# Fused attention and mixture of experts: the first expert's weight split planned behind the last gather, and a newly searched order of the experts' stage

## The chip, the cores and the metric

The kernel runs on one core of a Trainium2 chip. The metric is device time in microseconds (us) of one execution, the median of several. Engines: TensorE (PE; its weight loads are PEld), VectorE (DVE), ScalarE (ACT), GpSimd (POOL), and SyncE (SP), which issues most of the DMAs.

## The reference, cut to what matters

Two attentions feed a mixture of experts. The part that the change touches is the second function; its input `x` is the attention's output.

```python
def sm_attn(qq, kk, vv):            # softmax(scale * q k^T) v
    ...
p_packed = sm_attn(p, k, v)         # 8 x 8 heads, 32 packed rows
x = sm_attn(q, p_packed, p_packed)  # 8 x 8 heads, 576 rows -> 4608 tokens x 512

def _moe_ref(x, w_gate, w1, w2):
    N, D, E, cap = 4608, 512, 8, 576
    order = np.argsort(-(x @ w_gate).flatten())
    for idx in order:               # best (token, expert) pairs first
        tok, e = idx // E, idx % E
        if assigned[tok] >= 0 or counts[e] >= cap:
            continue
        assigned[tok] = e
        counts[e] += 1
    for e in range(E):              # w1[e]: 512 x 1024, w2[e]: 1024 x 512
        h = np.maximum(x[assigned == e] @ w1[e], 0)
        out[assigned == e] = h @ w2[e]
```

Each of the 8 experts gets exactly 576 tokens.

## The kernel before, in words

**Attention** runs first, in 16 groups of four heads. It writes `x` to DRAM (`xd`) and leaves the gate's logits on the chip (`Lg`). The change does not touch it.

**The router** finds the experts one after another, in the order in which they fill up. For expert n it masks what is taken (`close_a`, `close_b`, `build_a` to `build_v`), then narrows a threshold by counting steps: 2 for the first expert, 9 for the second, 11 for the others up to the seventh. One step is two counts on ScalarE (`count_a`, L868) and one on VectorE (`count_v`, L873), their sum over partitions on TensorE (`count_m`, L879 and L880), and the new threshold on VectorE (`upd_a`, L885, and `upd_b`, L894). `bound_m`, `test_m` and `assign` close the search. Then the list of the expert's 576 tokens is made: `slot_a` to `slot_v` and `onehot` on VectorE, the list products `list_m` (L1037) and `list_s` (L1049) on TensorE, and `list_b` (L1056), which leaves the indices in `gi`.

**An expert's rows** are fetched in five `gather`s (L1067), indirect DMAs that GpSimd issues: four of 128 rows and one of 64. For experts 0 to 2, TensorE transposes each piece (`xt_p`, L1100, into `px`), ScalarE rounds it to a high part `xh` (`xt_h`, L1106), and VectorE takes the low part `xl` from it (`xt_l`, L1111). For later experts the rows go through DRAM and VectorE transposes them (`xt_t` L1082, `xs_h`, `xs_l` L1094).

**An expert's weights** come in four quarters q, each a piece of `w1` and a piece of `w2` of 512 KB. SyncE loads them (`load`, L1120 and L1124), ScalarE makes the high part (`split_h`, L1129), and `split_l` (L1135) the low part. `split_l` is on GpSimd, in four instructions, but for the first quarter of expert 0, where VectorE does it in one instruction a piece. The loaded piece has two buffers, so quarter q + 2 can be loaded only when both splits of quarter q are done.

**The products** are f32 in three terms. `f1` (L1148) makes `hp` for one of eight slices f of the hidden size and one half m of the tokens: 4 matmuls of w1h by xh, 4 of w1h by xl, 4 of w1l by xh. `h_hi` (ACT, L1154) and `h_lo` (DVE, L1159) split the result, and `f2` (L1168 to L1173) adds to the five output tiles `y`. `ev` and `scatter` (L1201) write the rows out. `hp`, `px` and all small router products share three PSUM banks.

**The order** of all this is made when the program is built. Every operation of the experts' stage is entered in a planner (`Later`, a list scheduler) with an engine, a length (`LEN`), what it depends on, and a priority (a due time plus an entry of `TURN` for its kind and expert). The planner takes the operation that can start first; among those of one engine that can start at once it takes the one with the lowest priority. `SPARE` adds time between an operation on another engine and the named one. What comes out is the order in which each engine's queue is filled. Dependencies that stand only in the planner put nothing into the program: at run time an engine takes its queue in order and waits only where data or buffers ask for it. The planner thinks a gather landed 2.0 us after its issue plus .6 us, with 1.26 us between gathers, and puts `xt_p`, `xt_h`, `xt_l` some 1.6 us behind that.

Of the kernel before, what the change touches and what calls it, by code (L numbers as in the profile page):

```python
# [24 lines left out]
NTS = {1: 9}  # L25

LEN = {
    'assign': .4, 'bound': .08, 'bound_a': .1, 'bound_m': .14, 'build_a': 1.08, 'build_b': .72, 'build_k': 1.2, 'build_s': .13,
    'build_t': .15, 'build_v': .34, 'check_a': 1.6, 'check_m': .06, 'check_t': .6, 'close_a': .42, 'close_b': .48,
    'count_a': 1.2, 'count_m': .08, 'count_v': .44, 'ev': .48, 'ev_b': .6, 'expert': .09, 'f1': .533, 'f2': .7, 'f2x': .468,  # L30
    'gather': 1.26, 'h_hi': .31, 'h_lo': .38, 'list_a': .22, 'list_b': .6, 'list_m': .56, 'list_s': .22, 'load': .42,
    'member': .15, 'onehot': .67, 'scatter': 1.3, 'slot_a': .11, 'slot_b': .08, 'slot_c': .25, 'slot_d': .12, 'slot_e': .42,
    'slot_f': .42, 'slot_v': 1.4, 'split_h': .96, 'split_l': 2.8, 'test_c': .45, 'test_k': .28, 'test_m': .12, 'test_t': .2,
    'upd_a': .16, 'upd_b': .15, 'upd_c': .38, 'xg_ld': .5, 'xg_st': .38, 'xs_h': .42, 'xs_l': .47, 'xt_h': .48, 'xt_l': .6,
    'xt_p': .42, 'xt_t': .78}
# [243 lines left out]
def attention(ctx, tc, q, k, v, p, wg, xd, Lg, ident, wz, on_pool, early, late):  # L279
# [313 lines left out]


TURN = {
    'assign': (-9929.2, -1406.843, 695.138, 8016.483, 10766.841, 22037.982),
    'bound': (-3834.6, 19907.391, 1545.019, -15480.779, -5390.105, -3834.6),
    'bound_a': (0.0, -12064.251, -9565.382, -20090.433, -17648.964, 0.0),
    'bound_m': (0.0, -17844.652, -20096.332, -29653.072, -12440.691, 0.0),
    'build_a': (-2008.2, 18667.7, -18971.318, -5313.609, -5894.946, -2008.2),  # L600
    'build_b': (-2483.5, -7489.825, -13194.366, -4933.016, 4459.692, -2483.5),
    'build_k': (13240.5, 6770.915, 135183.815, 144824.42, 127860.865, 13240.5),
    'build_s': (0.0, -5506.748, 49376.469, 41829.641, 44711.332, 0.0),
    'build_t': (-9387.6, 18308.204, -24260.41, -19414.757, -22539.789, -9387.6),
    'build_v': (-8683.2, 3735.557, 34884.663, 34875.733, 36679.642, -8683.2),
    'check_a': (-3104.3, -3104.3, -3104.3, -3104.3, -3104.3, 25290.017),
    'check_m': (-3944.6, -3944.6, -3944.6, -3944.6, -3944.6, -8346.239),
    'check_t': (-3790.1, -3790.1, -3790.1, -3790.1, -3790.1, 3123.699),
    'close_a': (126.2, -22548.492, 259.466, 2123.26, 8359.189, 11624.021),
    'close_b': (-1960.4, 6234.801, 9449.371, 3539.501, 27866.288, -1960.4),  # L610
    'count_a': (-10221.0, 8707.999, -9829.586, -32227.368, -17557.572, -10221.0),
    'count_m': (-3687.4, 1429.069, -33012.921, -22925.971, -14518.958, -3687.4),
    'count_v': (-10658.5, -15050.716, -12417.95, 8192.386, -7906.393, -10658.5),
    'ev': (-5552.944, -3688.201, 6558.093, 8280.19, -10046.237, 13097.729),
    'ev_b': (-15492.946, 5184.873, 34456.107, 21302.216, 13334.529, -10138.807),
    'expert': (3457.5, -8328.201, 58298.188, 43236.934, 48338.711, 37867.42),
# [7 lines left out]
    'list_m': (16650.6, 15144.715, 2587.43, -12792.414, -3772.509, -20818.002),
    'list_s': (0.0, 27317.24, 3051.717, -3202.607, -457.014, 35078.358),
    'load': (24326.573, 97.039, -13710.125, -20482.231, -12447.259, 122.969),
    'member': (2847.3, 14117.27, 35484.901, 34707.856, 10795.168, 58872.233),
    'onehot': (-25997.2, -8211.351, -6183.93, -1931.135, 6932.093, -5368.273),
    'scatter': (10143.091, -36084.19, -8418.517, -10134.109, 5366.606, -12148.254),
    'slot_a': (-9633.1, -16932.437, 6718.434, -3983.583, -17178.811, -18985.786),  # L630
    'slot_b': (2288.0, -27923.294, 16326.799, -5139.904, 19811.628, -5998.061),
    'slot_c': (3152.9, -12181.673, 1877.318, -21791.852, -7757.971, -7053.733),
    'slot_d': (-1573.9, 29902.664, -5261.31, -22598.46, 12155.618, 8876.647),
    'slot_e': (-524.5, 2159.212, 37652.808, 34413.836, 34668.615, -8031.793),
    'slot_f': (7834.8, 15849.014, -9822.272, -628.14, -7972.32, 10427.988),
    'slot_v': (4056.3, 63995.495, 8187.024, -4230.816, 8863.725, 32775.272),
    'split_h': (3302.957, 59748.569, -127700.582, -128978.441, -133757.296, 20644.281),
    'split_l': (-7655.334, -5499.444, 36.831, 21635.26, 20988.04, 9614.49),
    'test_c': (1962.7, -53079.145, 3397.318, -7627.982, -17958.568, 1962.7),
    'test_k': (-9416.6, 18359.967, -60537.576, -65842.54, -78645.049, 6810.101),  # L640
    'test_m': (5327.7, 3430.116, -27468.576, -16199.522, -18112.833, 5327.7),
    'test_t': (-12609.4, -16891.226, 32800.306, 35251.939, 23245.714, -12609.4),
    'upd_a': (-7827.8, -25855.316, -15537.501, -3920.09, -18452.757, -7827.8),
    'upd_b': (1841.6, 13191.368, -13839.699, 7546.071, 18546.542, 1841.6),
    'upd_c': (40.5, -7739.416, 48363.268, 30737.669, 31194.472, 40.5), 'warm': (5018.43, 4200.7, 4200.7, 4200.7, 4200.7, 4200.7),
    'xg_ld': (-9296.7, -9296.7, -36445.1, -50675.93, -40479.904, 2433.332),
    'xg_st': (-1329.6, -1329.6, 3510.5, -3634.894, 20385.538, -26436.257),
    'xs_h': (-3606.4, -3606.4, -7756.0, -12318.781, 5109.768, -9563.927),
    'xs_l': (-45.1, -45.1, 19770.7, 16501.78, 19786.225, 3883.391),
    'xt_h': (-1214.368, -55658.344, 28097.803, 19354.6, 19354.6, 1824.8),  # L650
    'xt_l': (-4458.649, -10492.511, 30711.146, 15800.4, 15800.4, -9835.7),
    'xt_p': (-17602.312, 1842.144, 53034.826, 52713.8, 52713.8, 1446.9),
    'xt_t': (2153.2, 2153.2, -22396.6, -31796.512, -13888.503, -1010.97),}


def router_constants(nc, cst, tmp):
# [72 lines left out]
def experts(ctx, tc, rt, tmp, xd, xs, Lg, w1, w2, out, ident, wz, before):  # L729
# [549 lines left out]
    def u(k, f):  # L1279
        return 6.46 * (8 * k + f)  # L1280
# [15 lines left out]
    for n in range(E):  # L1296
# [5 lines left out]
        elif n:  # L1302
# [279 lines left out]
```

## Time and profile before

| what | value |
|---|---|
| median of 3 runs (lowest to highest) | 637.77 us (637.51 to 638.63) |
| the profiled execution | 643.15 us |
| its span, first to last instruction | 641.4 us |
| TensorE busy | 594.6 us (93%) |
| VectorE / ScalarE / GpSimd busy | 412.9 / 336.1 / 368.5 us |
| first `f1` matmul of expert 0 | 176.66 us |

The profile is one execution taken by the hardware profiler, with times from its first instruction. Attention fills about the first 148 us, the first expert's routing lies between 148 and 165 us, and the experts' stage after it. A busy TensorE need not be at its peak: matmuls are pipelined.

### The profile page before, as it was taken

Reading aid. Unit: us, or ns where it says so; the run is one execution under the profiler, and the core shown is the slowest. Engines: PE = TensorE matmul, PEld = TensorE weight load, DVE = VectorE, ACT = ScalarE, POOL = GpSimd, SP = SyncE. Lnnn points to the kernel's source line nnn. Section 1 sums busy time; section 2 is a strip of 40 time slices with the busy share of each in tenths; the row PEclk is TensorE's granted clock in tenths of the full one; section 3 lists DMA queues with packets and bytes.
Section 4 is the critical chain, followed back from the end, with each engine's and each line's share of the span. In section 5 each row is a group of like instructions: output and inputs, shape, how many; then the busy total and the mean of one; then the engine's idle time right before and its main releaser. Section 6 shows DMA issues by size and latency. Waiting matters only on the chain. (4 is left out here: it accounts for less than half of the span.)

```text
span 641.4 us, 12439 instructions
## 1 busy us (share of the span) xinstructions
PE 594.6 (93%) x4099; PEld 496.7 (77%) x4101; DVE 412.9 (64%) x1508; ACT 336.1 (52%) x853; POOL 368.5 (57%) x592
## 2 busy tenths in 40 slices
PE   6999899983699999999899999998999999999996
PEld 3678677752388888888788788797888989889984
DVE  7899999997666767657557966964792144162111
ACT  5677777762383774764664565385334235233102
POOL 8378676680570793962954783675447756725003
PEclk9899999997999999999999999999999999999998
DMA  8999996332820634432566365438333864812002
GB/s 274 369 341 309 296 319 198 111 112 75 269 68 6 226 107 150 155 108 76 196 231 155 132 214 116 141 137 245 103 100 107 261 157 144 241 44 75 1 1 78
DMA packets 76953, 103.42 MB, mean 161 GB/s; under 512 B 11792, under 2 KB 57104, under 8 KB 76880
## 3 DMA queue, kind: packets, MB, share of 16 engines
q1 hardware_dynamic: 70464, 83.64, 41.2%
q0 software_dynamic: 5888, 18.88, 8.5%
q8 instruction: 35, 0.57, 0.4%
q14 instruction: 38, 0.31, 0.2%
q10 hardware_dynamic: 528, 0.02, 0.1%
HBM read 77.74 MB, written 24.77 MB: 160 GB/s over the span
## 5 line engine op out<-in xcount | busy, mean ns | idle before, releaser
L1159 DVE SCALAR_TENSOR_TENSOR h<-hp,h 128x288 fp32r<-128x288 f32 (+2 forms) x192 | 59.5, 351 | 116.3 <-ACT h L1154 111.8
L1135 POOL TENSOR_TENSOR w2l<-w2s,w2h 128x256 fp32r<-128x256 f32 x124 | 92.0, 773 | 68.6 <-ACT w2h L1129 68.5
L1135 POOL TENSOR_TENSOR w1l<-w1s,w1h 128x256 fp32r<-128x256 f32 x124 | 91.1, 767 | 58.2 <-ACT w1h L1129 51.6
L1168 PE MATMUL y<-w2h,h 128*128 128x512 f32 x256 | 104.5, 408 | 0.0
L1170 PE MATMUL y<-w2h,h 128*128 128x512 f32 x256 | 101.0, 395 | 0.0
L1169 PE MATMUL y<-w2l,h 128*128 128x512 f32 x256 | 101.0, 395 | 0.0
L1148 PE MATMUL hp<-xh,w1h 128*128 128x288 f32 x512 | 91.5, 301 | 4.6 <-DVE h L1159 1.7
L1148 PE MATMUL hp<-xl,w1h 128*128 128x288 f32 x512 | 90.6, 299 | 0.6 <-DVE xl L1111 0.3
L1154 ACT ACTIVATE h<-hp 128x288 fp32r<-128x288 f32 x128 | 48.7, 406 | 80.4 <-issue 37.4
L1148 PE MATMUL hp<-xh,w1l 128*128 128x288 f32 x512 | 90.4, 298 | 0.0
L1148 PEld LDWEIGHTS hp<-xh,w1h 128*128 128x128 f32 x512 | 77.1, 188 | 10.8 <-DVE h L1159 1.7
L868 ACT ACTIVATE ja<-Vt,nT 128x288 bf16<-128x288 f32 x118 | 63.2, 536 | 36.7 <-DVE nT L894 34.5
L1148 PEld LDWEIGHTS hp<-xl,w1h 128*128 128x128 f32 x512 | 74.9, 188 | 1.3 <-DVE xl L1111 0.5
L1201 POOL DMA_INDIRECT out_dram<-xg,gi x40 | 39.1, 979 | 63.7 <-DVE fl L1427 36.9
L1148 PEld LDWEIGHTS hp<-xh,w1l 128*128 128x128 f32 x512 | 74.6, 188 | 0.1
L1129 ACT CAST w1h<-w1s 128x1024 fp32r<-128x1024 f32 x32 | 33.5, 1047 | 56.2 <-DMA w1s<-in_moe_w_dram 17.8
L1067 POOL DMA_INDIRECT xg<-xd,gi x40 | 39.0, 975 | 32.4 <-DVE Lw L989 21.7
L1170 PEld LDWEIGHTS y<-w2h,h 128*128 128x128 f32 x256 | 48.0, 187 | 11.5
L1169 PEld LDWEIGHTS y<-w2l,h 128*128 128x128 f32 x256 | 48.1, 188 | 8.2
L1168 PEld LDWEIGHTS y<-w2h,h 128*128 128x128 f32 x256 | 48.0, 188 | 8.3
L1129 ACT CAST w2h<-w2s 128x1024 fp32r<-128x1024 f32 x32 | 33.5, 1048 | 32.4 <-issue 13.3
L543 PE MATMUL xp<-P,th 128*128 128x264 f32 (+1 forms) x154 | 37.1, 329 | 7.0 <-ACT xs L553 4.5
(269 smaller groups left out, 1146.1 us busy)
## 6 DMA issues: line engine op xcount, KB each, us to landing
w1s<-in_moe_w_dram SPq DMA_DIRECT2D x32, 512.0 KB, 6.0
w2s<-in_moe_w_dram SPq DMA_DIRECT2D x32, 512.0 KB, 4.3
kl<-in_k_dram SPq DMA_DIRECT2D x16, 576.0 KB, 5.4
ql<-in_q_dram SPq DMA_DIRECT2D x16, 576.0 KB, 6.2
vl<-in_v_dram SPq DMA_DIRECT2D x32, 256.0 KB, 5.2
xd<-xs SPq DMA_DIRECT2D x32, 256.0 KB, 3.3
xg<-xs SPq DMA_DIRECT2D x20, 288.0 KB, 6.3
xs<-xg SPq DMA_DIRECT2D x20, 256.0 KB, 3.8
```

The costliest lines, as they stand in the source:

```text
L543: nc.tensor.matmul(xp[:m, :264], T[a, g][:, o:o + m], T[w, g], start=i == 0, stop=i == 2)
L868: nc.scalar.activation(ja, Vf, AF.Sign, bias=S_['nT'][:, j:j + 1], scale=-1.0, accum_out=cp[:, j:j + 1])
L1067: nc.gpsimd.indirect_dma_start(out=X['xg', k, c][:m], out_offset=None, in_=xd, in_offset=bass.IndirectOffsetOnAxis(ap=X['gi', k][:m, c:c + ...
L1129: nc.scalar.copy(X[n + 'h', k, q], X[n + 's', k, q])
L1135: eng.tensor_sub(X[n + 'l', k, q][r], X[n + 's', k, q][r], X[n + 'h', k, q][r].bitcast(F32))
L1148: nc.tensor.matmul(X['hp', k, f, n], X[W, k, q][:, d, 128 * r:128 * r + 128], X[Z, k][:, d, 288 * n:288 * n + 288], start=i + d == 0, stop ...
L1154: nc.scalar.activation(X['h', k, f][:, 288 * n:288 * n + 288], X['hp', k, f, n], AF.Relu)
L1159: V.scalar_tensor_tensor(h[:, o:o + b - a], p[:, a - 288 * n:b - 288 * n], 0.0, h[:, a:b].bitcast(F32), op0=OP.max, op1=OP.subtract)
L1168: nc.tensor.matmul(y, hh, wh, start=f == 0, stop=False)
L1169: nc.tensor.matmul(y, hh, wl, start=False, stop=False)
L1170: nc.tensor.matmul(y, hl, wh, start=False, stop=f == 7)
L1201: s = nc.gpsimd.indirect_dma_start(out=out, out_offset=bass.IndirectOffsetOnAxis(ap=X['gi', k][:m, t:t + 1], axis=0), in_=X['yo', k, t][:m ...
```

## The change

Three edits. First, the planner is told that `split_l` of expert 0's first quarter (the one on VectorE) depends on the last gather of expert 0; until now only the second and later quarters did. Second, lengths and spare times: the small products on TensorE are entered as .06 to .08 us longer, and .3 us of spare time is put in front of `count_m`, `bound_m`, `test_m`, `slot_a`, `slot_c`, `list_m`, `list_s` and `build_t`, .05 us in front of `f2`. Third, nearly all entries of `TURN` are new, the result of a search over orders with these settings. No instruction is added or removed; what changes is the order in each queue. The diff, cut to its core (58 lines of `TURN` have new numbers; four are shown):

```diff
 LEN = {
-    'assign': .4, 'bound': .08, 'bound_a': .1, 'bound_m': .14, 'build_a': 1.08, 'build_b': .72, 'build_k': 1.2, 'build_s': .13,
-    'build_t': .15, 'build_v': .34, 'check_a': 1.6, 'check_m': .06, 'check_t': .6, 'close_a': .42, 'close_b': .48,
-    'count_a': 1.2, 'count_m': .08, 'count_v': .44, 'ev': .48, 'ev_b': .6, 'expert': .09, 'f1': .533, 'f2': .7, 'f2x': .468,
+    'assign': .4, 'bound': .08, 'bound_a': .1, 'bound_m': .21, 'build_a': 1.08, 'build_b': .72, 'build_k': 1.2, 'build_s': .13,
+    'build_t': .22, 'build_v': .34, 'check_a': 1.6, 'check_m': .12, 'check_t': .6, 'close_a': .42, 'close_b': .48,
+    'count_a': 1.2, 'count_m': .14, 'count_v': .44, 'ev': .48, 'ev_b': .6, 'expert': .09, 'f1': .533, 'f2': .7, 'f2x': .468,
...
-SPARE = {'f1': .1, 'xt_p': .3}
+SPARE = {'f1': .1, 'f2': .05, 'xt_p': .3, 'count_m': .3, 'bound_m': .3, 'test_m': .3, 'slot_a': .3, 'slot_c': .3, 'list_m': .3, 'list_s': .3, 'build_t': .3}
...
-    'f1': (5538.963, 10905.075, 3567.902, -11602.304, -575.199, 10364.904),
-    'f2': (124988.012, 96881.814, 3574.469, -3442.054, 753.66, 15591.93),
+    'f1': (22829.595, 17476.141, -598.159, -17684.53, 8822.542, 16946.171),
+    'f2': (128367.327, 85925.544, -590.941, 1590.706, 15430.256, 20714.866),
...
-    'split_l': (-7655.334, -5499.444, 36.831, 21635.26, 20988.04, 9614.49),
+    'split_l': (-8891.522, 5752.33, 15284.995, 36562.132, 41772.256, 15822.959),
...
-    'xt_l': (-4458.649, -10492.511, 30711.146, 15800.4, 15800.4, -9835.7),
+    'xt_l': (-13398.275, -4227.517, 20493.449, 15800.4, 15800.4, -9835.7),
...
-                op(('split_l', n, q, w), e, d, zq, lambda n=n, q=q, w=w, eng=eng: split_l(n, q, w, eng), [('split_h', n, q, w)] + ([('gather', 0, 4)] if n == 0 and q else []))
+                op(('split_l', n, q, w), e, d, zq, lambda n=n, q=q, w=w, eng=eng: split_l(n, q, w, eng), [('split_h', n, q, w)] + ([('gather', 0, 4)] if n == 0 and q < 2 else []))
```

Read closely, the condition also changes for quarters 2 and 3 of expert 0: with `q` they were tied to the last gather, with `q < 2` they are not. Both follow quarter 1 on GpSimd, which stays tied.

## Rows read from the trace of the kernel before

**Rows 1.** Stretches of time: length, PE, PEld, DVE, ACT, POOL busy, PEclk, DMA.

```profile
176.60:629.60 453.00, 441.95 (x2773) 386.05 (x2773) 254.54 (x1076) 220.89 (x522) 249.06 (x349) 1.00 0.42 131
```

**Rows 2.** The same view in stretches of 16 us.

```profile
160.00:176.00 16.00, 10.31 (x56) 5.13 (x56) 10.43 (x28) 5.36 (x6) 8.76 (x10) 0.91 0.79 267
...
400.00:416.00 16.00, 14.94 (x83) 12.37 (x83) 15.86 (x34) 6.62 (x12) 9.74 (x13) 1.00 0.41 133
```

**Rows 3.** Timeline of PE at expert 0's start: start, duration, what, idle before.

```profile
169.77 0.63 PE L1100 MATMUL px<-ident,xg 128*128 128x128 f32 x4 [1.83 <-DVE wm L835]
...
175.33 0.66 PE L1100 MATMUL px<-ident,xg 128*128 128x128 f32 x4 [0.87 <-DMA xg<-xd,gi]
...
176.66 0.79 PE L1148 MATMUL hp<-xh,w1h 128*128 128x288 f32 x4
...
178.38 0.69 PE L1148 MATMUL hp<-xh,w1l 128*128 128x288 f32 x4
```

**Rows 4.** Timeline of POOL: the five gathers of expert 0.

```profile
166.00 1.20 POOL L1067 DMA_INDIRECT xg<-xd,gi  x1 [21.65 <-DVE Lw L989]
167.51 1.67 POOL L1067 DMA_INDIRECT xg<-xd,gi  x1 [0.30 <-issue]
169.48 1.04 POOL L1067 DMA_INDIRECT xg<-xd,gi  x1 [0.30 <-issue]
170.82 0.95 POOL L1067 DMA_INDIRECT xg<-xd,gi  x1 [0.30 <-issue]
172.07 0.91 POOL L1067 DMA_INDIRECT xg<-xd,gi  x1 [0.30 <-issue]
```

**Rows 5.** Timeline of DVE in the same stretch.

```profile
167.12 1.22 DVE L1135 TENSOR_TENSOR w1l<-w1s,w1h 128x1024 fp32r<-128x1024 f32 x1
168.25 1.22 DVE L1135 TENSOR_TENSOR w2l<-w2s,w2h 128x1024 fp32r<-128x1024 f32 x1
...
170.10 0.45 DVE L840 TENSOR_TENSOR ck<-eq,k 128x288 f32<-128x288 f32 x1
...
177.02 0.68 DVE L1111 TENSOR_TENSOR xl<-px,xh 128x512 fp32r<-128x512 f32 x1
```

**Rows 6.** Timeline of POOL: first and last of a later expert's five gathers.

```profile
496.47 0.98 POOL L1067 DMA_INDIRECT xg<-xd,gi  x1 [0.16 <-issue]
...
501.53 0.91 POOL L1067 DMA_INDIRECT xg<-xd,gi  x1 [0.30 <-issue]
```

**Rows 7.** Timeline of SP: loads of expert 0's quarters 2 and 3.

```profile
168.36 0.38 SPq L1120 DMA_DIRECT2D w1s<-in_moe_w_dram  x1
...
175.80 0.37 SPq L1120 DMA_DIRECT2D w1s<-in_moe_w_dram  x1
```

**Rows 8.** DMA queue of the gathers, 167.8 to 169.4 us: packets, MB, share.

```profile
q0 software_dynamic: 80, 0.26, 55.0%
```

**Rows 9.** DMA queue of the loads, 169.4 to 171.0 us.

```profile
q1 hardware_dynamic: 437, 0.45, 88.3%
```

**Rows 10.** Timeline of DVE beside a busy POOL, at 306 us.

```profile
306.24 0.99 DVE L840 TENSOR_TENSOR ck<-eq,k 128x288 f32<-128x288 f32 x1
```

**Rows 11.** Timeline of PE: expert 0's first f2, and its f1 for f = 4.

```profile
189.84 0.39 PE L1168 MATMUL y<-w2h,h 128*128 128x512 f32 x1
...
198.83 0.70 PE L1148 MATMUL hp<-xh,w1h 128*128 128x288 f32 x4
```

**Rows 12.** What PE waited for (176.6 to 640 us): total, times, longest.

```profile
PE pc L879 <- ACT ja L868: 3.8, 4, 2.4
...
PE pl L1037 <- DVE Bv L1027: 1.3, 2, 1.1
```

**Rows 13.** What DVE waited for, the same columns.

```profile
DVE g L885 <- remote: 5.7, 2, 4.4
```

**Rows 14.** Timeline of ACT: the first evacuation of expert 0's output.

```profile
243.11 0.58 ACT L1179 COPY xg<-y 128x512 f32<-128x512 f32 x1
```

**Rows 15.** Timeline of PE: the first f1 of expert 1.

```profile
234.10 0.80 PE L1148 MATMUL hp<-xh,w1h 128*128 128x288 f32 x4
```

More of the change, by code (lines that the diff above doesn't have):

```diff
@@ L27 @@
 LEN = {
[L28 to L33 removed]
+    'assign': .4, 'bound': .08, 'bound_a': .1, 'bound_m': .21, 'build_a': 1.08, 'build_b': .72, 'build_k': 1.2, 'build_s': .13,
+    'build_t': .22, 'build_v': .34, 'check_a': 1.6, 'check_m': .12, 'check_t': .6, 'close_a': .42, 'close_b': .48,
+    'count_a': 1.2, 'count_m': .14, 'count_v': .44, 'ev': .48, 'ev_b': .6, 'expert': .09, 'f1': .533, 'f2': .7, 'f2x': .468,
+    'gather': 1.26, 'h_hi': .31, 'h_lo': .38, 'list_a': .22, 'list_b': .6, 'list_m': .62, 'list_s': .3, 'load': .42,
+    'member': .15, 'onehot': .67, 'scatter': 1.3, 'slot_a': .18, 'slot_b': .08, 'slot_c': .32, 'slot_d': .12, 'slot_e': .42,
+    'slot_f': .42, 'slot_v': 1.4, 'split_h': .96, 'split_l': 2.8, 'test_c': .45, 'test_k': .28, 'test_m': .19, 'test_t': .2,
     'upd_a': .16, 'upd_b': .15, 'upd_c': .38, 'xg_ld': .5, 'xg_st': .38, 'xs_h': .42, 'xs_l': .47, 'xt_h': .48, 'xt_l': .6,
@@ L595 @@
 TURN = {
[L596 to L616, printed above, removed]
@@ L624 @@
[L624 to L630, printed above, removed]
@@ L651 @@
-    'xt_l': (-4458.649, -10492.511, 30711.146, 15800.4, 15800.4, -9835.7),
-    'xt_p': (-17602.312, 1842.144, 53034.826, 52713.8, 52713.8, 1446.9),
-    'xt_t': (2153.2, 2153.2, -22396.6, -31796.512, -13888.503, -1010.97),}
+    'assign': (-9929.2, 8021.767, 1598.018, 25071.993, 15905.586, 19528.151),
+    'bound': (-3834.6, 33362.577, 23308.579, -14054.897, 4294.231, -3834.6),
+    'bound_a': (0.0, -23099.862, -18927.01, -6646.28, -7446.145, 0.0),
+    'bound_m': (0.0, -16262.41, -25858.1, -29606.998, -6444.35, 0.0),
@@ new lines @@
+    'build_a': (-2008.2, 13932.591, -19234.405, 477.463, -21918.238, -2008.2),
+    'build_b': (-2483.5, 6419.326, -19940.965, -13355.792, -3326.46, -2483.5),
+    'build_k': (13240.5, 21336.957, 103092.436, 142588.696, 138208.467, 13240.5),
+    'build_s': (0.0, -1424.652, 62993.037, 30494.077, 42436.465, 0.0),
+    'build_t': (-9387.6, 15342.024, -22513.891, -35046.8, -27715.647, -9387.6),
+    'build_v': (-8683.2, -5257.386, 26835.481, 34680.713, 39948.709, -8683.2),
+    'check_a': (-3104.3, -3104.3, -3104.3, -3104.3, -3104.3, 43347.295),
@@ new lines @@
+    'check_m': (-3944.6, -3944.6, -3944.6, -3944.6, -3944.6, -6322.488),
+    'check_t': (-3790.1, -3790.1, -3790.1, -3790.1, -3790.1, -15637.835),
+    'close_a': (126.2, -19872.0, 3529.0, -4647.709, 16010.75, 15146.648),
+    'close_b': (-1960.4, 13714.184, 9752.643, 6162.018, 35035.524, -1960.4),
+    'count_a': (-10221.0, 34463.865, -16869.524, -38255.921, -13828.885, -10221.0),
+    'count_m': (-3687.4, 19119.637, -21950.979, -25841.009, -13216.544, -3687.4),
+    'count_v': (-10658.5, -18579.112, -1973.712, 15307.119, -3064.439, -10658.5),
@@ new lines @@
+    'ev': (-5262.78, 8732.876, -3312.21, 13749.653, 2483.229, 8455.869),
+    'ev_b': (-20778.526, 10758.981, 42803.284, 19365.779, 12982.825, -25592.823),
+    'expert': (3457.5, -12565.341, 59526.876, 36408.156, 55063.13, 37630.649),
+    'f1': (22829.595, 17476.141, -598.159, -17684.53, 8822.542, 16946.171),
+    'f2': (128367.327, 85925.544, -590.941, 1590.706, 15430.256, 20714.866),
+    'gather': (-19807.898, -17526.384, 26831.228, 6211.744, 16258.338, -10318.461),
+    'h_hi': (-7203.688, 8190.046, -24358.184, -32127.244, -38725.715, 1091.569),
@@ new lines @@
+    'h_lo': (144985.247, 36211.178, -120910.825, -129786.648, -102869.948, -8767.126),
+    'list_a': (-5736.9, 3506.348, -2894.641, -21125.526, -5240.8, 11358.32),
+    'list_b': (-4287.7, -4602.215, 21828.469, 21153.02, 10476.004, -2393.23),
+    'list_m': (16650.6, -1866.812, 8825.717, -12769.88, -20082.349, -27825.146),
+    'list_s': (0.0, 31015.054, -1423.308, -8724.485, -2031.368, 43162.251),
+    'load': (29195.964, -5213.228, -20105.183, -22848.27, 10482.923, 5317.691),
+    'member': (2847.3, 1657.626, 28105.959, 19702.891, 11131.417, 42301.767),
@@ new lines @@
+    'onehot': (-25997.2, -4637.029, 4617.025, 17324.255, 18155.693, -7134.441),
+    'scatter': (-3079.539, -36319.851, -15381.982, -4717.305, -12046.487, -7488.892),
+    'slot_a': (-9633.1, -29016.499, 6916.409, 1763.574, -28259.36, -25042.797),
+    'slot_b': (2288.0, -37339.746, 7038.655, -7776.758, 39752.884, -9947.809),
+    'slot_c': (3152.9, 2587.544, 15779.572, -27765.095, -2425.377, -6279.842),
+    'slot_d': (-1573.9, 42703.399, -16354.488, -20152.432, 43124.918, 11807.561),
+    'slot_e': (-524.5, -12362.447, 32778.061, 35681.945, 42120.073, -13170.635),
@@ new lines @@
+    'slot_f': (7834.8, 19508.334, 3740.097, 13227.229, -14056.57, 412.734),
+    'slot_v': (4056.3, 52116.547, 7005.684, -9821.897, 2272.477, 33003.907),
+    'split_h': (1539.77, 51266.657, -130841.756, -118788.835, -136425.023, 3870.087),
+    'split_l': (-8891.522, 5752.33, 15284.995, 36562.132, 41772.256, 15822.959),
+    'test_c': (1962.7, -43103.917, -3277.242, -16950.572, -16166.007, 1962.7),
+    'test_k': (-9416.6, 27275.419, -64604.854, -60036.051, -85175.115, -2132.716),
+    'test_m': (5327.7, 4068.44, -31485.699, -22332.481, -15709.744, 5327.7),
@@ new lines @@
+    'test_t': (-12609.4, -7291.335, 34765.673, 29793.034, 24125.08, -12609.4),
+    'upd_a': (-7827.8, -20526.605, -19341.518, -4060.258, -15045.112, -7827.8),
+    'upd_b': (1841.6, 6711.31, -10709.151, 6628.116, 13161.676, 1841.6),
+    'upd_c': (40.5, -18236.017, 47908.396, 36301.817, 44165.171, 40.5), 'warm': (9197.001, 4200.7, 4200.7, 4200.7, 4200.7, 4200.7),
+    'xg_ld': (-9296.7, -9296.7, -36445.1, -49281.95, -52762.719, 6863.685),
+    'xg_st': (-1329.6, -1329.6, 3510.5, -3114.488, 18960.125, -28569.847),
@@ L656, in router_constants @@
+    'xs_h': (-3606.4, -3606.4, -7756.0, -17440.144, -4743.496, -28153.478),
+    'xs_l': (-45.1, -45.1, 19770.7, 23186.09, 14135.45, 9355.42),
+    'xt_h': (8029.526, -49095.055, 32048.864, 19354.6, 19354.6, 1824.8),
+    'xt_l': (-13398.275, -4227.517, 20493.449, 15800.4, 15800.4, -9835.7),
+    'xt_p': (-22839.794, 4857.71, 51927.149, 52713.8, 52713.8, 1446.9),
+    'xt_t': (2153.2, 2153.2, -22396.6, -37154.31, -5140.819, -12055.573),}
 def router_constants(nc, cst, tmp):
```

24 lines of the change are left out of this document (removed).

## The prediction, made before the change was run

> **What bounds the kernel now.** First I read the engines' busy times over the experts' stage, from the first `f1` to the last product [rows 1]. TensorE is busy in 441.95 of 453.00 us; the other engines reach 255 us at most. So TensorE's queue sets the end, and a change of order alone can win in two ways: let this stretch begin earlier, or take something from the 453.00 - 441.95 = 11.05 us in which TensorE stands still inside it.
>
> Next come the stretches of 16 us [rows 2]. In 160 to 176 us TensorE is busy only 10.31 us. In 400 to 416 us it is VectorE that is full, 15.86 of 16 us, while TensorE falls to 14.94. There the end is set by VectorE, which matters for a rival below.
>
> Then the start, in time order. The third piece of rows is transposed at 175.33, after a wait for a DMA, and the first `f1` follows 1.33 us later at 176.66 [rows 3]. So the gathers are late. Their issues show where from [rows 4]: the second took 1.67 us where the last took .91, and it lies under VectorE's two splits, 167.12 to 169.47 [rows 5]. A later expert's five gathers, with little beside them, take 501.53 + .91 - 496.47 = 5.97 us [rows 6]; expert 0's take 172.07 + .91 - 166.00 = 6.98 us. The loads tell the rest [rows 7]: the load of quarter 2 is issued at 168.36, right as the first split (167.12 + 1.22) gives its buffer back. Without other traffic a gather moves its .26 MB in some 1.6 us [rows 8]; in the following 1.6 us the weights alone have the DMA engines, .45 MB [rows 9]. So the early splits hurt the gathers twice: in the issue, and by calling loads in front of them.
>
> **The change part by part.**
>
> *The split's new place.* Nothing is removed: VectorE still spends 2 x 1.22 us on the two splits, and two loads stay as large as they were. What moves is their place. By the planner's own figures the split is ready .6 us after the last gather lands, `xt_l` of a piece some 2.2 us after its own gather lands, and gathers stand 1.26 us apart. So `xt_l` of the third piece is ready .3 us before the split and that of the fourth .9 us behind it. I take it that the first split stands behind the third piece's `xt_l`.
>
> The gathers: the third one's issue ends at 169.48 + 1.04 = 170.52 now. With clean spacing it would end at 166.00 + 3 x 1.26 - .30 = 169.5; with the other VectorE work in that stretch still beside it (the first and third gathers took 1.20 and 1.04), at 166.00 + 1.20 + .30 + 1.04 + .30 + 1.04 = 169.9. From the first gather's end (167.20) to its transpose (169.77) it is 2.57 us [rows 3, 4]. That gives 172.1 to 172.5 for the third transpose. If the pieces queue at 1.6 us each behind the first, landed at 169.4 [rows 8], it is 169.4 + 3.2 + .4 = 173.0. I take 172.8, 2.5 us before 175.33.
>
> The first `f1` then starts at 174.1, and the third piece's `xl`, which ends at 177.02 + .68 = 177.70 now [rows 5], ends at 175.2. Behind it come the split, 1.22 us, and a price for GpSimd, which by then works on its own splits: beside a busy GpSimd the same VectorE instruction took .99 us against .45 [rows 5, 10], so +.54. w1l is ready at 175.2 + 1.22 + .54 = 177.0, and the third group of `f1`, now at 178.38, starts at 177.05: **1.3 us earlier**. Bounds: if the split falls into VectorE's idle time before that `xl`, the whole 2.5 us stay; if it stands behind the fifth piece's `xl` (landing 169.4 + 4 x 1.6 - .8 = 175.0, plus .4 to the transpose, plus the 177.70 - 175.33 = 2.37 from transpose to end of `xl`), w1l is ready at 177.8 + 1.76 = 179.5, 1.1 us later than now.
>
> The second split is needed by the first `f2`, at 189.84 [rows 11]; it ends near 179, ten us of cover. The loads of quarter 2 go out 8.6 us later, at 177.0, and meet those of quarter 3 (175.80). Their weights are first used at 198.83, so 20 us of casts and GpSimd splits cover them. Were this cover gone, the price would be those 8.6 us.
>
> *The Trainium skill speaks against the first half of this.* Its page "SBUF — State Buffer", section "Who interferes with whom", says that a VectorE tensor_tensor with two SBUF inputs contends with GpSimd's reads but does not stall the issue of GpSimd's DMAs, since writing descriptors needs the other interface (which the page calls inferred). By that rule the 1.67 us would have another cause and stay. The rows disagree: of the five gathers the long ones are those under such instructions, 1.67 us under the splits, and the free one took .91.
>
> *Slack in front of small products.* TensorE waited 3.8 us for counts in 4 waits, 2.4 of it in one, and 1.3 us for the list products [rows 12]. The long one follows a stop of VectorE, 4.4 us for something that the profile can't name [rows 13]; slack doesn't cover that. What .3 us of slack can address is 3.8 - 2.4 + 1.3 = 2.7 us. Bounds are nothing and 2.7; I take **1.5 us**: five waits are left (three for counts, two for lists) and each can get .3 us shorter.
>
> *The new priorities.* They move everything else in the queues. Of 11.05 us of idle time 11.05 - 3.8 - 1.3 = about 6 belong to other waits. I have no row for how the new order spends them: zero, with half of it, 3 us, either way. The stop of VectorE may go or come back elsewhere: zero, 2.4 us either way.
>
> *The f2 slack and the lengths* move no instruction by themselves beyond this.
>
> Sum: 1.3 + 1.5 = 2.8 us. The profiled execution, 643.15 us (its span of 641.4 and 1.75 around it), would become 640.35. It lies 5.4 us above the median of the runs, 637.77; I take the same 2.8 us from that: **635.0 us**. A change within .2%, 1.3 us, can't be told from none.
>
> **The rivals.**
>
> *More than forecast.* The split fits before the third `xl` (2.5), the slack closes all its waits (2.7), and VectorE's long stop goes (2.4): 7.6 us, 630.2. For it: the same stop appears only twice [rows 13], so it hangs on circumstance. Against: three good ends at once.
>
> *Given back.* TensorE gains at the start, but at expert 4 VectorE is full [rows 2], and TensorE had already run short there. If VectorE's work there starts no earlier, since the router paces it and not TensorE, the 2.8 us are lost again: 637.8. For it: 15.86 of 16. Against: VectorE is busy only 255 of 453 us, so the plan has room ahead of it.
>
> *The gather is not held by the split.* The second gather's 1.67 us has another cause, and only the loads' move helps. Then the third gather's issue still ends at 170.52, its transpose comes at about 173.3 and the start gains .8 instead of 1.3: 635.5. This is what follows from the skill's page above. The long issues under the splits speak against it [rows 4, 5].
>
> *Slower: the slack lengthens the router.* In the plan each counting step gets .36 us longer (.3 and .06) and seven other products .37 each: 11 x .36 + 7 x .37 = 6.6 us for an expert. At expert 1 there is cover: TensorE begins its `f1` at 234.10 and still finishes expert 0's products until 243.11 [rows 14, 15], up to nine us of stock. At expert 4 there is none [rows 2]. If its rows come the whole 6.6 us later, the time is 637.77 - 2.8 + 6.6 = 641.6; it decides for slower from 2.8 + 1.3 = 4.1 us of delay. Against it: the slack only delays where TensorE would have waited anyway, and with VectorE busy in 255 of 453 us most stretches have room for it [rows 1].
>
> **How the numbers follow.** Forecast .42, own range 632.5 to 636.4 (the terms half a bound either way). More than forecast .13. Gather not held .10. Given back .20, of which .03 reach beyond +.2%. Slower .15. Faster by over .2%: .42 + .13 + .10 = .65; within: .17; slower: .03 + .15 = .18. The range goes from just under the first rival's time, where the free order adds a little (629.5), to halfway into the slower one (639.5); about .07 lie below it and .12 above.
>
> **What would show it.** Right: no gather of expert 0 over 1.25 us, the fifth issue ending before 172.5; loads of quarter 2 issued after 175; the third transpose near 172.8 and the third group of `f1` near 177; TensorE's waits for counts and list products under 3 us together. Wrong: that group at 178.4 or later with a wait for w1l; TensorE's idle time after its first `f1` above 11 us; a wait for `xl` or `xh` near expert 4; a longer stop of VectorE that no instruction of the program explains.

## The result, and the profile after

The change made the kernel slower. Its median is 641.28 us (639.10 to 650.77, 15 runs) against 637.77 us (634.75 to 639.87, 15 runs): ratio **1.0056, 95% interval 1.0036 to 1.0076**. Forecast were 635.0 us and faster; the time lies outside the range too. The profiled execution took 639.84 us, its span 637.9.

The start went as forecast. In the timeline of GpSimd (POOL) no gather takes more than 1.20 us (1.67 in [rows 4]):

```profile
166.22 1.20 POOL L1067 DMA_INDIRECT xg<-xd,gi  x1 [21.41 <-DVE Lw L989]
167.73 0.96 POOL L1067 DMA_INDIRECT xg<-xd,gi  x1 [0.30 <-issue]
...
171.51 0.91 POOL L1067 DMA_INDIRECT xg<-xd,gi  x1 [0.30 <-issue]
```

In the timeline of SyncE (SP) the load of quarter 2's first piece is issued at 175.24 instead of 168.36 [rows 7]. The line takes in two loads; the second, quarter 3's, is at 177.11:

```profile
175.24 2.24 SPq L1120 DMA_DIRECT2D w1s<-in_moe_w_dram  x2
```

In TensorE's timeline the third transpose is at 173.02 (forecast 172.8), the first `f1` at 175.02 and the third group at 177.14 (forecast 177.05; [rows 3] had 175.33, 176.66, 178.38):

```profile
173.02 0.60 PE L1100 MATMUL px<-ident,xg 128*128 128x128 f32 x4
...
175.02 0.79 PE L1148 MATMUL hp<-xh,w1h 128*128 128x288 f32 x4 [0.16 <-DVE xl L1111]
...
177.14 0.79 PE L1148 MATMUL hp<-xh,w1l 128*128 128x288 f32 x4 [0.22 <-DVE w1l L1135]
```

VectorE's (DVE) splits took 1.87 and 1.56 us instead of 1.22 each [rows 5]:

```profile
175.21 1.87 DVE L1135 TENSOR_TENSOR w1l<-w1s,w1h 128x1024 fp32r<-128x1024 f32 x1
...
178.56 1.56 DVE L1135 TENSOR_TENSOR w2l<-w2s,w2h 128x1024 fp32r<-128x1024 f32 x1
```

So every sign that the prediction named for a right start came. The loss lies later. In the stretch from the first `f1` to the last product TensorE was busy 445.76 of 456.40 us, so it stood still 10.64 us, against 11.05 in [rows 1]. The columns are length, then busy us (instructions) of PE, PEld, DVE, ACT, POOL, then PEclk, DMA share, GB/s:

```profile
175.00:631.40 456.40, 445.76 (x2791) 387.16 (x2791) 262.04 (x1079) 224.59 (x525) 256.18 (x358) 1.00 0.43 133
```

The first profile of before was a poor measure for that: its 11.05 us held VectorE's 4.4 us stop [rows 13], which neither after nor the next profile has. In that next one, of the same kernel (the first experiment), TensorE stood still 451.85 - 446.05 = 5.80 us:

```profile
178.45:630.30 451.85, 446.05 (x2795) 389.69 (x2795) 255.81 (x1078) 222.66 (x525) 251.84 (x355) 1.00 0.43 132
```

Its third group starts at 180.19 (TensorE's timeline), 12.93 us after its first gather at 167.26; in the first profile that distance was 178.38 - 166.00 = 12.38 us, so it varies by half a microsecond between profiles of one kernel:

```profile
180.19 0.69 PE L1148 MATMUL hp<-xh,w1l 128*128 128x288 f32 x4
```

Where after has its 10.64 us shows in the table of waits of TensorE from 300 us to the end (what waited, for what; us, times, longest), 8.2 us together:

```profile
PE pl L1037 <- DVE Bv L1027: 2.3, 1, 2.3
PE pl L1037 <- DVE h L1159: 1.8, 2, 1.4
PE pc L879 <- ACT ja L868: 1.0, 1, 1.0
PE hp L1148 <- DVE gi L1056: 0.9, 1, 0.9
PE pv L850 <- DVE h L1159: 0.9, 1, 0.9
PE plw L1049 <- DVE h L1159: 0.6, 1, 0.6
PE psl L995 <- DVE mb L960: 0.4, 1, 0.4
PE hp L1148 <- DVE xl L1094: 0.3, 1, 0.3
```

The same table for the second profile of before has 3.2 us:

```profile
PE pl L1037 <- DVE Bv L1027: 1.4, 2, 1.1
PE pc L879 <- ACT ja L868: 0.8, 1, 0.8
PE hp L1148 <- DVE g L885: 0.5, 1, 0.5
PE hp L1148 <- DVE xl L1094: 0.3, 1, 0.3
PE hp L1148 <- DVE h L1159: 0.2, 1, 0.2
```

The products that got slack wait more, not less: list products (`pl`, `plw`) 4.7 us instead of 1.4, and the key transpose (`pv`) and the slot product (`psl`), which did not wait before, 1.3. Counts (1.0) and list products come to 5.7 us, where the prediction's sign for being right was under 3; yet none of its signs for being wrong came (10.64 us is just under its 11).

### The profile page after: what moved, and what is told of

The parts are those of the page before. It is cut to its first block, busy times and chain, and to the rows that moved or that the text cites. A ratio compares the mean times of both kernels' runs of the same rounds, so it can differ in the third digit from the quotient of the medians.

```text
span 637.9 us, 12425 instructions
## 1 busy us (share of the span) xinstructions
PE 594.1 (93%) x4101; PEld 495.3 (78%) x4101; DVE 418.0 (66%) x1508; ACT 337.4 (53%) x853; POOL 370.6 (58%) x592
## 4 chain that ended last, share of the span: by engine, by line
PE 55%; DVE 8%; DMA 5%; issue 2%; POOL 1%; ACT 1%; SPq 0%; POOLq 0%; DVEq 0%; ACTq 0%
PE hp L1148 26%; PE y L1168 8%; PE y L1169 7%; PE y L1170 7%; DMA w1s<-in_moe_w_dram 2%; PE y L1172 2%; PE y L1173 2%; DMA w2s<-in_moe_w_dram 2%; DVE xt L1082 1%; DMA xg<-xd,gi 1%; PE px L1100 1%; POOL out_dram L1201 1%; DVE h L1159 1%; DVE xl L1094 1%; PE pl L1037 1%
## 5 line engine op out<-in xcount | busy, mean ns | idle before, releaser
L1135 POOL TENSOR_TENSOR w1l<-w1s,w1h 128x256 fp32r<-128x256 f32 x124 | 93.3, 784 | 58.5 <-ACT w1h L1129 55.2
```

Source lines behind the costliest of these rows:

```text
L1135: eng.tensor_sub(X[n + 'l', k, q][r], X[n + 's', k, q][r], X[n + 'h', k, q][r].bitcast(F32))
```

## The experiments

Kernels that keep a searched order but for a few steps have this at their end. It takes the planner's order and puts each named step right behind its anchor, so that all other queues stay as they were:

```
def emit_moved(self):
    o = self.schedule()[0]
    for k, a in MOVES:
        o.remove(k)
        o.insert(o.index(a) + 1, k)
    for k in o:
        self.ops[k][2]()
Later.emit = emit_moved
```

**Both kernels again** (no edit), each timed beside before like all others.

> The kernel before once more, unchanged, for a second profile. Theory A (the profiled execution of before was an unlucky one, and what it showed as idle was partly chance): the span is near 636 us, VectorE's unexplained stop of 4.4 us is gone or elsewhere, and TensorE's idle time after its first f1 is 5 to 8 us instead of 11. Theory B (the profile was typical): span 640 to 642 with the same waits in the same places.

> The changed kernel once more, unchanged. Theory A (the new order itself costs some 5 us, the new start gives some 2 back): median 640 to 642 us, 3 to 4 us above before, and the second profile shows the same long waits for list products near 424 and 486 us. Theory C (the clock: in many of its executions TensorE has one more stretch at half clock): the granted clock falls from .984 to .976 in the slower runs, and the runs at .984 are no slower than before.

Before: 638.09 us, ratio .9994 (.9976 to 1.0011), without VectorE's stop. After: 643.41 us, ratio 1.0075 (1.0048 to 1.0103). In this second profile of after the start is bad: VectorE's split took 4.21 us instead of 1.87, TensorE waited 2.55 us for w1l, and from 181.90 to 185.30 its granted clock was .50, that is 1.2 instead of 2.4 GHz. From 300 us on it waited 8.0 us, as in the first. VectorE's and GpSimd's timelines:

```profile
176.65 4.21 DVE L1135 TENSOR_TENSOR w1l<-w1s,w1h 128x1024 fp32r<-128x1024 f32 x1
```

```profile
176.99 2.78 POOL L1135 TENSOR_TENSOR w2l<-w2s,w2h 128x256 fp32r<-128x256 f32 x4
```

Theory C, the clock, holds only in part. In the first timing after's runs at a granted clock of .976 to .980 took 641.28 to 644.84 us and the four at .984 only 639.10 to 639.84; but before's seven runs at .983 to .986, timed again, took 636.51 to 638.26. So at a like clock after is still the slower one.

**The move alone, and all but the move.** The first takes the order of before and moves only the two splits, the loads that their buffers call, and the casts of these:

```
MOVES = [(('split_l', 0, 0, 1), ('xt_l', 0, 2)), (('load', 0, 2, 1), ('split_l', 0, 0, 1)),
         (('split_l', 0, 0, 2), ('upd_a', 1, 0)), (('load', 0, 2, 2), ('split_l', 0, 0, 2)),
         (('split_h', 0, 2, 1), ('h_hi', 0, 1, 0)), (('split_h', 0, 2, 2), ('h_hi', 0, 0, 1))]
```

The second takes the order of after and puts the splits and their loads back:

```
MOVES = [(('split_l', 0, 0, 1), ('split_h', 0, 0, 2)), (('split_l', 0, 0, 2), ('split_l', 0, 0, 1)),
         (('load', 0, 2, 1), ('split_l', 0, 0, 1)), (('load', 0, 2, 2), ('split_l', 0, 0, 2))]
```

> Before's order with only the two VectorE splits of expert 0, the two loads that wait for them and the two casts of those loads moved to where the changed kernel has them. Theory A: the start gain of some 2 us stays to the end, 635 to 636 us. Rival D (the later splits and loads cost as much downstream as the gathers win): 638 us or more. Theory C: no change in the clock, as TensorE's queue is the same.

> The changed kernel's order with only the two splits and their loads put back in front of the gathers, as before has them. Theory A: the start gain is lost, 643 to 644 us. Rival D: 638 to 640 us, faster than the changed kernel.

The move alone: 639.72 us, ratio 1.0034 (1.0015 to 1.0053). All but the move: 643.57 us, ratio 1.0088 (1.0061 to 1.0115). So the new order costs some 5.6 us (.0088 x 638.2) without the move, and the move alone, forecast at -1.3, costs some 2. The two don't add up to after, which lies at 1.0056 and 1.0075: in the order of after the move gains .8 to 2.0 us, which is within the intervals. In the trace of the move alone the third group comes 10.23 us after the first gather (168.30 to 178.53), where before needed 12.93 (12.38 in its first profile): the start did gain over 2 us. It went away at once. VectorE's second split stands ahead of `h`, TensorE waits for `h`, and then computes at half clock for 3.41 us, at most 1.7 us of work lost (TensorE's timeline, then the stretches, whose PEclk is .50):

```profile
182.34 1.07 PE L1148 MATMUL hp<-xh,w1h 128*128 128x288 f32 x4 [2.08 <-DVE h L1159]
```

```profile
182.66:186.07 3.41, 3.41 (x17) 3.26 (x16) 1.88 (x11) 0.43 (x2) 0.00 (x0) 0.50 0.80 266
```

The timed runs fit that: their median granted clock is .975, against .982 for before beside them.

**VectorE's second split later, twice.** As the move alone, but `('split_l', 0, 0, 2)` stands behind `('h_lo', 0, 1, 0)`. This kernel, the first with GpSimd's splits, the one with six products later and the first with slack alone ran on a chip on which before took 646.20 us; the first two of them were run again on another.

> As the kernel that moves the splits alone (639.72 us, ratio 1.0034), but VectorE's second split, w2l, stands behind h of the second group instead of ahead of h of the first. Theory (that split holds h, h holds TensorE for 2.08 us, and the half clock follows the wait): the wait for h falls below 1.1 us, no stretch at half clock near 182, ratio to before .998 to 1.001, 637 to 638.5 us. Rival (the price is the collision with GpSimd's splits and the wait for w1l): unchanged, 639 to 640 us, ratio 1.002 to 1.005.

> The splits' move alone with VectorE's second split behind the second h, once more (ratio 1.0017, interval .9981 to 1.0053). Theory (the second split ahead of h caused the wait and the half clock, and these ate the gain): .997 to 1.000, the wait for h at 1.0 us, full clock from 164 us on. Rival (VectorE's first split beside GpSimd's is the price by itself): 1.002 to 1.004, as when both splits are moved.

1.0017 (.9981 to 1.0053), then 1.0016 (.9990 to 1.0042): above the theory's .998 to 1.001 and .997 to 1.000, just under the rivals' 1.002. Nothing is gained, and whether less is lost than with both splits moved (1.0034) can't be told. The two profiles show why the price of the first split isn't a number, though the two engines' records start within .08 us of each other in both; who was ahead is read from the lengths. In the first, VectorE goes ahead, and its split takes 1.22 us (DVE's timeline):

```profile
176.12 1.22 DVE L1135 TENSOR_TENSOR w1l<-w1s,w1h 128x1024 fp32r<-128x1024 f32 x1
```

GpSimd's four parts take 3.87 us (POOL's timeline):

```profile
176.12 3.87 POOL L1135 TENSOR_TENSOR w2l<-w2s,w2h 128x256 fp32r<-128x256 f32 x4
```

In the second, GpSimd goes ahead: VectorE's split takes 3.93 us (DVE's timeline),

```profile
176.05 3.93 DVE L1135 TENSOR_TENSOR w1l<-w1s,w1h 128x1024 fp32r<-128x1024 f32 x1
```

GpSimd's parts take 2.76, undisturbed (POOL's timeline),

```profile
176.13 2.76 POOL L1135 TENSOR_TENSOR w2l<-w2s,w2h 128x256 fp32r<-128x256 f32 x4
```

and TensorE waits 3.05 us for the result (PE's timeline), and has half its clock from 181.20 to 188.00:

```profile
180.03 0.80 PE L1148 MATMUL hp<-xh,w1l 128*128 128x288 f32 x4 [3.05 <-DVE w1l L1135]
```

**GpSimd makes both splits, three forms.** If the two engines' splits collide, one engine should make them all. The order is that of before; the splits move to GpSimd, w1l behind the fifth gather and w2l behind quarter 1's w1l:

```
- eng, e, d = (V, 'DVE', 1.16) if n + q == 0 else (nc.gpsimd, 'Pool', 2.95)
+ eng, e, d = (nc.gpsimd, 'DVE', 1.16) if n + q == 0 else (nc.gpsimd, 'Pool', 2.95)
MOVES = [(('split_l', 0, 0, 1), ('gather', 0, 4)), (('load', 0, 2, 1), ('split_l', 0, 0, 1)),
         (('split_l', 0, 0, 2), ('split_l', 0, 1, 1)), (('load', 0, 2, 2), ('split_l', 0, 0, 2)),
         (('split_h', 0, 2, 1), ('h_hi', 0, 1, 0)), (('split_h', 0, 2, 2), ('h_hi', 0, 0, 1))]
```

> The order of before; GpSimd makes both splits of expert 0's first quarter, w1l right behind its fifth gather, w2l behind its split for the second quarter's w1l; the loads and casts of quarter 2 are moved as in the kernel that moves the splits alone. Theory (the two engines' splits collide, and VectorE's splits then stand ahead of h): w1l is ready 2.8 us after the fifth gather's issue, before the third group of f1 asks for it; nothing stands ahead of h on VectorE, so the 2.1 us wait for h and the 3.4 us at half clock behind it don't come. The third group starts 9.5 us after the first gather (10.24 with VectorE's splits moved, 12.94 before), TensorE stands still at most 6 us behind its first f1, and the time is 635.5 to 636.5 us, ratio .996 to .998 to before. Rival (VectorE's other work paces the start anyway): the same start as before, ratio 1.000. Rival (GpSimd, with 5.6 us more to do, brings the next quarters' weights late): a wait for w1l or w2l of quarter 1 or 2 on TensorE, ratio above 1.002.

> The first kernel with GpSimd's splits once more (ratio .9996, interval .9969 to 1.0023, on a chip on which before took 646 us), now without the two later changes that the kernel at .9945 had. Theory (the start's gain is real, two waits for counts of 1 us take part of it): .996 to .998. Rival (without those two changes nothing is gained): .999 to 1.001.

.9996 (.9969 to 1.0023) on the slower chip, then .9977 (.9958 to .9996). The collision is gone, but ScalarE's casts of quarter 2 now stand ahead of two pairs of counts (TensorE's timeline of the second run):

```profile
183.68 0.16 PE L879 MATMUL pc<-cp,same 128*128 128x3 f16 x1 [1.03 <-ACT ja L868]
...
187.58 0.16 PE L879 MATMUL pc<-cp,same 128*128 128x3 f16 x1 [0.95 <-ACT ja L868]
```

The next form mends that:

```
-        (('split_l', 0, 0, 2), ('split_l', 0, 1, 1)),
+        (('split_l', 0, 0, 2), ('load', 0, 2, 1)),
-        (('split_h', 0, 2, 1), ('h_hi', 0, 1, 0)),
+        (('split_h', 0, 2, 1), ('xt_h', 0, 4)),
```

> As the kernel in which GpSimd makes both splits of expert 0's first quarter in the order of before, with two changes read from its trace: GpSimd makes w2l right behind w1l, so that quarter 2's second load goes out 2.8 us earlier, and ScalarE's cast of quarter 2's w1 stands ahead of the second h, in idle time, instead of ahead of the second pair of counts. Theory (the early start is kept if no engine pays for it): the two waits for counts of 1.03 and .98 us behind the casts go, the third group of f1 still starts 9.4 to 9.6 us after the first gather, TensorE is some 3.5 us ahead of before at expert 0's end, and the ratio to before is .994 to .998. Rival (the start isn't what sets the end, the router of expert 1 is): ratio .999 to 1.001. The kernel without these two changes gave .9996.

**634.36 us against 638.19, ratio .9945 (.9925 to .9965)**: faster than both kernels of this study. w1l is made in 2.79 us right behind the gathers and w2l in 2.80, the third group follows 9.57 us after the first gather (166.09 to 175.66) without a wait for w1l, and the waits for counts at 183 to 188 are gone. POOL's timeline:

```profile
172.31 2.79 POOL L1135 TENSOR_TENSOR w1l<-w1s,w1h 128x256 fp32r<-128x256 f32 x4
175.06 2.80 POOL L1135 TENSOR_TENSOR w2l<-w2s,w2h 128x256 fp32r<-128x256 f32 x4
```

And PE's:

```profile
175.66 0.69 PE L1148 MATMUL hp<-xh,w1l 128*128 128x288 f32 x4
```

Over the rest TensorE stands still 451.80 - 446.28 = 5.52 us, as before does (5.80), so nothing is given back: the 3.4 us (12.93 - 9.57; 2.8 by the first profile) reach the end, as the 3.5 us of the ratio say.

```profile
173.90:625.70 451.80, 446.28 (x2796) 389.82 (x2795) 256.10 (x1078) 222.91 (x525) 260.36 (x367) 1.00 0.44 135
```

**This start in the order of after.** The same line and the first four moves of that kernel, applied to after.

> After's order, but GpSimd makes both splits of expert 0's first quarter right behind its fifth gather (w1l, w2l, then quarter 2's loads), as in the kernel that beat before with ratio .9945; nothing else of after is touched. Theory (two separate things: the move collides with GpSimd, the priorities cost 3 to 5 us at experts 3 to 7): the start gains what the collision took, 1.5 to 3 us against after, no half clock near 182 and no wait for w1l, and the waits at experts 3 to 7 stay: ratio to before .999 to 1.003. Rival (the searched priorities were fit for VectorE's split and lose as much without it): 1.005 to 1.009, as after. Rival (the start was all of after's loss): .995.

641.77 us, ratio 1.0057 (1.0026 to 1.0087). The start is good (third group 10.29 us after the first gather, no wait for w1l), and from 300 us on TensorE waits 8.6 us. So after's loss doesn't lie in the start. The ratio is that of the rival, not the .999 to 1.003 of the theory: the better start is worth little here. Against the profile with the splits put back, the third group comes 3.15 us earlier behind the first gather (10.29, 13.44), the last instruction only 1.2 us earlier behind it (472.55, 473.74).

**Six products later.** The order of after; the products that it waited for stand one to four groups later, for example for expert 7's list products:

```
MOVES = [
...
    (('f1', 5, 3, 1, 0), ('h_lo', 5, 2, 1)), (('f1', 5, 3, 1, 1), ('f1', 5, 3, 1, 0)),
    (('f1', 5, 3, 1, 2), ('f1', 5, 3, 1, 1)), (('f2', 5, 0, 4), ('f1', 5, 3, 1, 2))]
```

> The order of after, but six of the products that TensorE waited for in all its profiles stand one to four groups later in TensorE's queue: the transpose of expert 4's keys, the list products of experts 4, 5 and 7 (by 1, 3 and 4 groups), expert 6's first slot product and its last list product. Theory (the searched order puts these products where their inputs aren't there yet; the waits are the loss): of 6.0, 4.7 and 4.5 us of such waits in the three profiles 1 us is left, TensorE stands still 6 to 7 us behind its first f1 instead of 10.4 to 12.4, and the time falls by 3.5 to 4.5 us to 637 to 638 us, ratio to before 1.000. Rival (VectorE is late as a whole, and another product waits in their place): 640.5 us or more, ratio 1.004 or more.

1.0084 (1.0044 to 1.0123): the theory fell. The waits for list products from 300 us on sink from 4.7 to .5 us, but counts now wait 5.4, `f1` 3.4 for `h`, and the second slot product 1.1. On that chip two kernels with the order of before wait 2.5 and 3.3 us for counts there too (the first with GpSimd's splits, and the second split later), so part of the 5.4 may be the chip's; the ratio, to before on the same chip, holds. What remains as an explanation, not shown by itself: a product queued later lets the router go on later, and its next product is missing.

**Slack without new priorities, two ways, and priorities without slack.** First 89 of the 94 products of experts 2 to 7 each change places with the next group of `f1` or `f2` in the order of before. Then the planner's tables are exchanged, `LEN` and `SPARE` of before in after, and those of after in before; both replan the whole order (the lengths differ by .06 to .08 us for the same products, not shown):

```
-SPARE = {'f1': .1, 'f2': .05, 'xt_p': .3, 'count_m': .3, 'bound_m': .3, 'test_m': .3, 'slot_a': .3, 'slot_c': .3, 'list_m': .3, 'list_s': .3, 'build_t': .3}
+SPARE = {'f1': .1, 'xt_p': .3}
```

> The order of before, but 89 of the 94 counts, bounds, tests, slots and list products of experts 2 to 7 stand one group of f1 or f2 (.53 to .7 us) later in TensorE's queue; everything else as before: slack without new priorities. Theory of the prediction's second term: the waits for counts and lists in the repeated profile of before (.77, .24 and 1.13 us) go and nothing else comes, 636 to 637 us, ratio .997 to .999. Rival (slack lengthens the router by 18 times .55 us, some 10 us for an expert, and its rows come later): a wait for xl, xh or a turned row block at experts 4 to 7, 640 to 644 us, ratio 1.003 or more.

> After without its slack: the lengths and the slack of before (LEN, SPARE), the priorities and the dependence of after. Theory (the slack makes the router longer, and that is the 5 us): ratio to before .999 to 1.002, against 1.0056 and 1.0075 for after. Rival (the searched priorities themselves make the longer order): 1.005 to 1.010, as after.

> Before with the lengths and the slack of after (LEN, SPARE), and the priorities and the dependence of before. Theory (slack removes waits for counts and lists): ratio to before .997 to 1.000. Rival (slack lengthens the router, as 89 products one group later did, at 1.0089): 1.005 or more, with waits for xl, h or list products at experts 3 to 6.

Slack alone: 1.0089 (1.0053 to 1.0125). TensorE waits 2.2 us for `xl` and 2.2 us for list products (from 300 us on):

```profile
PE hp L1148 <- DVE xl L1094: 2.2, 1, 2.2
PE pl L1037 <- DVE Bv L1027: 2.2, 1, 2.2
```

After without slack: 641.50 us, 1.0051 (1.0027 to 1.0075), as after. Its profile has 4.8 us of waits from 300 us on, and those for list products are .6 instead of after's 4.7 (the three longest):

```profile
PE hp L1148 <- DVE h L1159: 1.8, 1, 1.8
PE pc L879 <- ACT ja L868: 0.8, 1, 0.8
PE pl L1037 <- DVE Vt L856: 0.6, 1, 0.6
```

But it waits 2.23 us for w1l at the start (TensorE's timeline), with half clock from 179.81 to 183.22 behind it, and has half clock once more from about 487.0 to 490.4, behind the wait of 1.8 us for `h`:

```profile
178.85 0.80 PE L1148 MATMUL hp<-xh,w1l 128*128 128x288 f32 x4 [2.23 <-DVE w1l L1135]
```

Before with the slack's tables: 654.76 us, 1.0232 (1.0195 to 1.0269), on the rival's side (1.005 or more), with 13.2 us of waits from 300 us on.

## Why the prediction was wrong

**The step that failed** is the pair of terms on the order: "Slack in front of small products", 1.5 us to be won, and "The new priorities. ... I have no row for how the new order spends them: zero, with half of it, 3 us, either way." Together they were forecast to win 1.5 us; they cost some 5. On the chips where before takes 638 us, four profiles with the order of after have about 8 us of waits from 300 us on (8.2, 8.0, 8.1 with the splits back, 8.6 with GpSimd's), and the five with the order of before that followed the first have about 3 (3.2 before, 3.3 the move alone, 3.0, 3.1 and 3.1 the later forms). That is 5.1 us, and the ratios agree: 1.0088 without the move is 5.6 us; 1.0057 against .9977, both with GpSimd's splits at the start, is 5.1, and against .9945, whose four moves it has, 7.1 on another chip. (The first profile of before has 8.0 us too, with VectorE's stop; its 643.15 us lay above all 15 timed runs of before.)

How the 5 us divide between slack and priorities is not settled. Undoing the slack returned nothing that the times can tell (1.0051), and expert 4's rows are late without it too: its first gather comes 212.7 us behind expert 0's, 209.8 to 213.5 in the four profiles of after's order, 202.6 to 207.8 in the five of before's. But without the slack the waits for list products are nearly gone, and 1.0051 can't be told from the 1.0034 of the move alone; its bad start may hide a gain.

Why the inputs come late in that order can be read at its longest wait, for expert 7's list products. VectorE builds them while GpSimd splits weights, and its small instructions are stretched (DVE's timeline in the profile of after):

```profile
481.67 0.60 DVE L1014 TENSOR_SCALAR s2i<-sl 128x36 int32<-128x36 int32 x1
482.19 0.78 DVE L1015 TENSOR_SCALAR s2i<-sl 128x36 int32<-128x36 int32 x1
483.00 0.67 DVE L1016 CAST sbf<-s2i 128x72 bf16<-128x72 int32 x1
...
485.28 1.28 DVE L1031 TENSOR_TENSOR A<-sbf,iob 128x1152 bf16<-128x1152 bf16 x1
```

Beside them POOL's timeline has

```profile
480.80 2.82 POOL L1135 TENSOR_TENSOR w2l<-w2s,w2h 128x256 fp32r<-128x256 f32 x4
483.58 3.57 POOL L1135 TENSOR_TENSOR w1l<-w1s,w1h 128x256 fp32r<-128x256 f32 x4
```

and TensorE's the wait:

```profile
487.96 0.74 PE L1037 MATMUL pl<-Bv,A 128*128 128x144 bf16 x9 [2.29 <-DVE Bv L1027]
```

In the second profile of before the first three have an idle GpSimd beside them:

```profile
466.44 0.17 DVE L1014 TENSOR_SCALAR s2i<-sl 128x36 int32<-128x36 int32 x1
466.53 0.17 DVE L1015 TENSOR_SCALAR s2i<-sl 128x36 int32<-128x36 int32 x1
466.73 0.20 DVE L1016 CAST sbf<-s2i 128x72 bf16<-128x72 int32 x1
```

The three take 2.05 us instead of .54, 1.5 us more, five times the .3 us that the slack allows. From the first of them to `Bv` the list's instructions take 5.81 us instead of 3.20, 2.6 us more, about as much as the wait of 2.29. This is one place; that contention makes all the late inputs was argued from it, not shown, and the kernel with six products later speaks for a router that is late as a whole, not one product.

**The start: mechanism right, price mis-sized.** The gathers, their transposes and the third group came as forecast; the load came 1.8 us before its forecast, right behind GpSimd's split of quarter 1 (172.44 + 2.77 = 175.21): it did not wait for VectorE's split, though the prediction had it so. The price "for GpSimd ... so +.54" was wrong in kind: over seven profiles with VectorE's first split in its new place it took 1.22, 1.57, 1.87, 2.95, 2.96, 3.93 and 4.21 us, so 0 to 3.0 us more, 1.5 on the mean. Whoever goes first holds the other, for up to the whole of its work. The Trainium skill says as much on its page "SBUF — State Buffer", section "Who interferes with whom": a VectorE instruction with two SBUF inputs contends with a GpSimd instruction that reads SBUF, and the order of issue decides who is blocked. The traces agree (1.22 us beside 3.87, 3.93 beside 2.76). Missing was also what follows: in four profiles, behind a wait for w1l or for `h` of 2.1 to 3.1 us, TensorE lost half its clock for 3.4 to 6.8 us, and the second split holds `h`. So the move's -1.3 became some +2 in the order of before. In the order of after it came out near the forecast, .8 to 2.0 us, and that is partly luck: the split took 1.87 us in one profile there and 4.21 in the next. The prediction weighed the skill's section only for the old place of the splits.

**The gather not held by the split** fell. The second gather took 1.67 and 1.66 us in the two profiles of before 1.67 with the splits put back into after's order and in both kernels with slack on before's order, and .96 in both profiles of after, in the move alone and in the kernel at .9945. No run moves the splits without the loads; but in the stretch of [rows 8] that holds most of this issue one packet of a load ran beside 80 of the gathers.

**Slack, -1.5,** didn't come. The waits for list products grew instead, and the rival's mechanism ("the slack lengthens the router") is real: products queued one group later cost 1.0089 on the order of before, with TensorE waiting 2.2 us for `xl`. The result lies close to this rival's 641.6 us, but not by its path alone: after's rows for expert 4 come 4 to 7.5 us later, yet TensorE waits for list products and only .3 us for `xl`, and after without slack is as slow.

**Given back** fell in the order of before: the kernel at .9945 keeps its whole start to the end. In the order of after, GpSimd's splits kept only 1.2 of 3.15 us, by one profile each.

**The base.** The forecast drew its gains from a profile that had 4.4 us more of VectorE's stop than the next one; of 11.05 us to win only 5.80 were there in the next.

**Open** are why the searched order puts the router where it does, how much of the 5 us is slack and how much priorities, and how much of the waits is contention.

## What to carry to other kernels

When an instruction is moved, look up who uses the same memory ports in the new place, and price the meeting by both orders of arrival, not by a mean; giving both pieces of work to one engine can beat the faster engine. A new order, from new priorities and slack, was the largest part of this change, not a zero: allow for a loss as large as the gain that is hoped for. And profile the kernel before twice before counting what is to be won.

## What the runs showed of the hardware that was not expected

VectorE's split of 1.22 us took 3.93 and 4.21 us and ended 1.09 us after the last of GpSimd's four instructions in a row: it waited for all of them, not for one. TensorE's clock fell to .50 behind waits of 2.08, 2.23, 2.55 and 3.05 us near 180 us, and not in the profiles where the longest wait there was 1.0 to 1.3 us. The length of the wait alone doesn't decide: it also fell behind 1.8 us at 485.50 (after without slack), and behind 2.22 us for a gather at 170.39 (after) it stayed at 1.00. VectorE's stop of 4.37 us in the first profile of before came again with 4.42 us at the same instruction (L885, 440.16) in one kernel on the slower chip (another there stopped 3.00 us at this instruction, put down to TensorE), and in none of the five later profiles with that order on the others; what it waits for stays open.
